# Idle TensorE products in the first block of a delta-rule and feed-forward kernel: 25 in place of 16 behind the first inverse, and seven more in the block's solve

## The chip, the cores and the metric

One core of a Trainium2 chip runs the whole kernel. The metric is the device time of one execution in microseconds (us). A trace of one profiled execution of the kernel before is at hand; the times quoted beside it are of executions without the profiler.

## What is computed

For 4 sequences of 8 heads, 768 steps and 48 channels a delta rule is run, and its output goes through a feed-forward layer. Cut to what matters:

```python
k_n = k / (norm(k) + 1e-6)
for t in range(S):                                   # S = 768
    y[t] = einsum('bhd,bhde->bhe', q[t], state)
    v_old = einsum('bhde,bhd->bhe', state, k_n[t])
    state = state + beta[t] * outer(k_n[t], v[t] - v_old)
x = y as (3072, 384)
h = x @ w_in                                         # 384 x 2048
out = maximum(0.01 * h, h) @ w_out                   # 2048 x 384
```

## The kernel before

The 768 steps are cut into 12 blocks of 64. A block's steps are not run one by one: the Gram products of its keys make a triangular system, this system is inverted (`inv`), and the inverse gives all 64 outputs of the block by matrix products (`solve`). The inverse of blocks 0 and 1 is made together, by elimination on VectorE (DVE, lines 387 and 392), and stands at the front of the program, since nothing else can start before it. All later inverses run beside the feed-forward products of earlier blocks.

In `solve(0)` TensorE (PE) and ScalarE (ACT) take turns, for each of two groups `g` of heads: the corners of the inverse (`pz` L506, `pu` L541, 32 x 32 products, each followed by an ACT copy), the new values (`pw` L635, copied to `rv` by ACT at L637), and the outputs (`py` L655, copied to `ys` by ACT at L657). `columns(0)` turns the outputs by six TensorE transposes (`px` L690), ACT copies them to `x` (L695), and `ffn(0)` multiplies `x` by the feed-forward weights: `ph` (L721), then the activation `gh` on ACT (L731), then `po` (L712).

The weights arrive as raw 64-bit words (`wr`, line 133) and are made into float32 beside block 0's work, one of eight parts `j` after the other: `pack` (ACT, L148), `conv` (DVE, L158 to L161), `expand` (ACT, L168), `final` (DVE, L175), for later blocks also `cast` (ACT, L182) and `lows` (DVE, L189). A table `work` says after which step of block 0 each of these is written, and some carry a gate: `pack(3)` may start only behind the first activation `gh`, `expand(0)` behind the copies to `rv` and `ys`. The engines take their instructions in the order written out, after a scheduling pass has sorted them by its own estimate of when each is ready. A change in one place can so move rows on every engine further on.

One thing on PE has no effect on any result. `warm`, called while the elimination of blocks 0 and 1 still runs (with 12 steps to go), multiplies a constant tile `neg` (128 x 128) by itself, 512 columns wide, 16 times, into a PSUM tile that is not read. These are the idle products. In the kernel before they stand at line 399, and there are no others.

Of the kernel before, what the change touches and what calls it, by code (L numbers as in the profile page):

```python
# [31 lines left out]
HC = C // 2  # L32
P = 128
# [14 lines left out]
def delta_moe_kernel(ctx: ExitStack, tc, kq0, kqT, kv, qT, beta, cst, w_all, out, nblk):  # L48
# [10 lines left out]
    nc = tc.nc  # L59
# [25 lines left out]
    neg = st.tile([P, P], F32R, name="neg")  # L85
# [111 lines left out]
    def need(gen, fn, n):  # L197
        while (fn, n) not in done:
            next(gen)
# [194 lines left out]
    def warm(x, count):  # L394
# [3 lines left out]
        for i in range(count):  # L398
            nc.tensor.matmul(ps.rearrange("p (o t) -> p o t", t=P), neg,
                             neg.rearrange("p (o t) -> p o t", o=1).broadcast_to([P, 4, P]), start=True, stop=True)  # L400

    def inv(b):

        if b:
            need(gg, gram, NB[b][0])
        two = len(NB[b]) > 1
        M = HC if two else HC // 2
        X = sb.tile([P, HC * HC], F32, tag="T", name=f"T{b}", bufs=1)
        T = X[:, 0:M * HC].rearrange("p (m i) -> p m i", m=M)
        if two:  # L410
            nc.gpsimd.memset(T, 0.0)
        else:
            with behind("gl"):
                nc.vector.memset(T, 0.0)
        yield
        L = Lh.pop(b)
        c = norms(b, L.rearrange("p m i -> p (m i)")[:, ::HC + 1])
        if two:
            nc.vector.tensor_copy(X[:, ::HC + 1], c)
        else:  # L420
            for e in range(2):
                r = slice(e * 64, e * 64 + 64)
                nc.vector.tensor_copy(X[r, e:M * HC:HC + 2], c[r, e::2])
        for x in range(2):
            l = L[:, x * HC // 2:(x + 1) * HC // 2]
            nc.vector.tensor_tensor(l, l, c.rearrange("p (o i) -> p o i", o=1).broadcast_to(list(l.shape)), ALU.mult)
        if two:
            for n in NB[b]:
                lengths(n)
        yield  # L430
        for j in range(HC - 1):
            eliminate(b, L, j, T, j + 1 if two else j // 2 + 1)
            if two and j in WARM:
                warm(T[:, 0], WARM[j])
            if j == HC - 2:
                if two:
                    Tc = sb.tile([P, HS, HC], F32, tag="L", name="tc", bufs=2)
                    nc.vector.transpose(Tc.rearrange("p l i -> p i l"), T.rearrange("p m i -> p i m"))

                    for i, n in enumerate(NB[b]):  # L440
                        Tts[n] = Tc, T[i * 64:i * 64 + HC]
                    for g in range(NGR):
                        place(0, g, 1)
                    d = nc.vector.transpose(T, T)
                    mark["inverse"] = d.ins
                    for g in range(NGR):
                        d = place(0, g, 0)
                    mark["inverse"] = d.ins
                else:
                    n = NB[b][0]  # L450
                    Tt = X[:, M * HC:].rearrange("p (i m) -> p i m", m=M)
                    nc.scalar.copy(Tt.rearrange("p i m -> p m i"), T)
                    td = dr.tile([2, HC, HS, HC], F32, tag="td", name=f"td{n}")
                    tt = dr.tile([HS, HC, HC], F32, tag="tt", name=f"tt{n}")
                    Tts[n] = td, tt
                    for x in range(2):
                        a = x * 64
                        for e in range(2):
                            nc.sync.dma_start(td[e, x::2].rearrange("m l i -> l m i"), T[a + e * HS:a + (e + 1) * HS])
                        nc.sync.dma_start(tt.rearrange("l i (x m) -> x l i m", m=M)[x], Tt[a:a + HS])  # L460
                done.add((inv, b))
                if b == 1:
                    mark["el2"] = mark["steps"]
            yield
# [119 lines left out]
    def solve(n):  # L584
        b = where[n][0]
        need(iv, inv, b)
        if n not in nts:
            with behind("po"):
                lengths(n)
        nt = nts.pop(n)  # L590

        def load(g):
            merge_z(n, g, tv(n, g))
            if 0 < n < 3:
                fetch(n, g)

        def tie(g):
            merge_u(n, g, tv(n, g))

        def heads(rows):  # L600

            return ((c, u, slice(c * 64, c * 64 + rows)) for u in range(GU) for c in (1, 0))

        def quarters():

            return ((c, u, e) for u in range(GU) for c in range(2) for e in range(2))

        def out_of(x, g, w):
            p = ps_a.tile([P, 512], F32, tag="a", name=f"{x}{n}_{g}")
            return p[:, 0:GU * w].rearrange("p (u t) -> p u t", u=GU)  # L610

        def kt(g):

            t, k, v = tv(n, g), of("k", n, g), of("v", n, g)
            if n:
                pv = out_of("pk", g, C)
                for c, u, r in heads(D):
                    nc.tensor.matmul(pv[r, u], k[DN, c, u], t[DN, c, u // NPAIR, u % NPAIR], start=True, stop=True)  # L618
                for c in range(2):
                    nc.scalar.mul(t[UP, c], pv[c * 64:c * 64 + D].rearrange("p (y v) t -> p y v t", y=2), -1.0)  # L620
            if not n:
                return
            for s in range(GS):
                us = slice(s * NPAIR, (s + 1) * NPAIR)
                with behind("gl"):
                    nc.vector.tensor_tensor(
                        v[DN, :, us], v[DN, :, us],
                        nt[DN, g, :, us].rearrange("p h (u o) -> p h u o", o=1).broadcast_to([C, 2, NPAIR, D]), ALU.mult)

        def step_w(g):  # L630
            t, v = tv(n, g), of("v", n, g)
            pv = out_of("pw", g, D)
            for c, u, e in quarters():
                a = c * C + e * HC
                nc.tensor.matmul(pv[a:a + HC, u], t[:, c, u // NPAIR, u % NPAIR, e * HC:(e + 1) * HC], v[:, c, u], start=True, stop=True)  # L635
            for c in range(2):
                d = nc.scalar.copy(v[DN, c], pv[c * 64:c * 64 + C])  # L637
            mark["rv"] = d.ins

        def step_s(g):  # L640
            k, v, v1 = of("k", n, g), of("v", n, g), of("v", n + 1, g)
            pv = out_of("pc", g, D)
            for c, u, r in heads(D):
                with nullcontext() if n else behind("ph"):
                    nc.tensor.matmul(pv[r, u], k[:, c, u], v[:, c, u], start=True, stop=True)  # L645
            for c in range(2):
                nc.scalar.copy(v1[UP, c], pv[c * 64:c * 64 + D])  # L647

        def step_y(g):

            qa, v = of("q", n, g), of("v", n, g)
            pv = ps_a.tile([P, 512], F32, tag="a", name=f"py{n}_{g}")
            for c, u, e in quarters():
                a = (c ^ (u // NPAIR)) * C + e * HC
                nc.tensor.matmul(pv[a:a + HC, u * D:(u + 1) * D], qa[:, c, u, e * HC:(e + 1) * HC], v[:, c, u], start=True, stop=True)  # L655
            ys[n, g] = y = sb.tile([P, DO], F32, tag="ys", name=f"ys{n}_{g}", bufs=3)
            mark["ys"] = nc.scalar.copy(y, pv[:, 0:DO]).ins  # L657
            if not n and not g:
                expand(0, "ys", slice(1, 2))

        stages = [(0, load), (1, tie), (LD, kt), (LD + 1, step_w), (LD + 2, step_y), (LD + 3, step_s)]
        if n in (0, nblk - 1):
            stages.remove((LD + 3, step_s))
        for s in range(NSLOT):
            for g in range(NGR):
                for at, stage in stages:
                    if at == s:
                        stage(g)
            if s == NSLOT - 1:
                done.add((solve, n))  # L670
                if 1 < n < nblk - 1:
                    for g in range(NGR):
                        fetch(n + 1, g)
                if n == 0:
                    columns(0)
                    yield
                    for g in range(NGR):
                        step_s(g)
            yield


    def columns(n):

        need(sv, solve, n)
        xs[n] = parts = []
        px = [ps_a.tile([P, 2, TB], F32, tag="a", name=f"px{n}_{i}") for i in range(2)]
        part = [px[cc // 2][:, cc % 2] for cc in range(NCC)]
        for cc, x in enumerate(part):
            for g in range(NGR):
# [155 lines left out]


WEARLY, NPACK, NG = 4, 3, 5
WARM = {HC - 12: 16}
KA = 2
IV, GG = ((9, 17), (6, 17), (6, 17), (2, 17)), ((2, 4), (1, 2), (1, 2))  # L850
SV = (0, 10), (3, 13), (1, 11), (2, 12)
# [67 lines left out]
```

## Time and profile before

| what | value |
|---|---|
| runs without the profiler | 623.45 us median of 3 (622.75 to 623.54) |
| the profiled execution's own time | 627.45 us |
| its span, first to last instruction | 625.7 us |
| mean granted TensorE clock over the span | 0.983 |
| busy share of PE, DVE, ACT | 93%, 69%, 53% |

Busy time is the union of an engine's instructions. The granted clock is 1.00 where TensorE runs at 2.4 GHz and 0.50 where it runs at 1.2 GHz; there is no level between, and a fraction means that the level changed inside the stretch. Ahead of its first record of the clock the profile prints 1.00; there the pace of the products tells the level.

### The profile page before, as it was taken

The numbers are of one execution on the slowest core, as the hardware profiler recorded it, in microseconds if no ns is written. First come the engines' busy times: TensorE is split into PE (matmuls) and PEld (weight loads), VectorE is DVE, ScalarE is ACT, GpSimd is POOL, SyncE is SP. The second block draws the span as 40 slices with busy tenths as digits, with TensorE's granted clock in tenths as the row PEclk, the third lists the DMA queues.
The fourth block names the chain that finished last, engine by engine and source line by source line (L and its number), as shares of the span: only waits on it lengthen the run. The fifth ranks groups of instructions, "written<-read, shape, count | busy, mean of one in ns | idle before, by whom it ended". The sixth has DMA issues, their size and how long they took to land.

```text
span 625.7 us, 22323 instructions
## 1 busy us (share of the span) xinstructions
PE 583.0 (93%) x9122; PEld 534.8 (85%) x9122; DVE 431.2 (69%) x1949; ACT 330.0 (53%) x818; POOL 33.6 (5%) x61
## 2 busy tenths in 40 slices
PE   5279989889899989999999999999999999999996
PEld 4267766689888989999999989999999999999996
DVE  3997899969739949759659739749749659431212
ACT  3475976735536436545545536536545545454432
POOL 6000000100010010010010010010010010100100
PEclk9986999989999999999999999999999999999999
DMA  5986932262266570581580571570580550410101
GB/s 124 310 262 224 282 79 66 43 129 32 46 114 126 103 136 12 104 145 20 106 156 6 110 136 22 113 140 15 112 152 4 114 100 4 85 28 4 25 1 26
DMA packets 122022, 59.69 MB, mean 95 GB/s; under 512 B 111296, under 2 KB 112384, under 8 KB 120896
## 3 DMA queue, kind: packets, MB, share of 16 engines
q1 hardware_dynamic: 117056, 52.95, 39.4%
q0 software_dynamic: 2112, 4.33, 2.7%
q8 instruction: 72, 1.18, 0.9%
q10 hardware_dynamic: 2752, 0.98, 0.8%
q14 instruction: 30, 0.25, 0.1%
HBM read 46.96 MB, written 11.27 MB: 93 GB/s over the span
## 4 chain that ended last, share of the span: by engine, by line
PE 73%; DVE 13%; DMA 5%; ACT 5%; issue 3%; SPq 2%; DVEq 0%; ACTq 0%
PE ph L721 28%; PE po L712 27%; PE pk L618 3%; PE pw L635 3%; DVE T L392 3%; DVE tmp L387 3%; PE py L655 3%; PE pc L645 3%; PE pg L306 2%; DVE w L189 1%; PE px L690 1%; DMA gd<-gs 1%; DMA sq<-tt 1%; ACT cg L168 1%; PE pu L489 1%
## 5 line engine op out<-in xcount | busy, mean ns | idle before, releaser
L721 PE MATMUL ph<-xh,w 128*128 128x256 f32 x1056 | 205.6, 286 | 0.5 <-issue 0.5
L712 PE MATMUL po<-w,gh 128*128 128x384 f32 x704 | 177.9, 344 | 0.0
L721 PEld LDWEIGHTS ph<-xh,w 128*128 128x128 f32 x1056 | 169.2, 189 | 4.8 <-issue 3.9
L736 DVE TENSOR_TENSOR gl<-ph,gh 128x256 fp32r<-128x256 f32 x176 | 74.0, 421 | 143.0 <-ACT ph L735 133.8
L731 ACT ACTIVATE gh<-ph 128x256 fp32r<-128x256 f32 (+1 forms) x192 | 73.5, 385 | 181.9 <-PE ph L721 121.8
L721 PE MATMUL ph<-xl,w 128*128 128x256 f32 x528 | 149.0, 284 | 1.7 <-DVE xl L124 1.7
L712 PEld LDWEIGHTS po<-w,gh 128*128 128x128 f32 x704 | 120.9, 188 | 3.4 <-issue 1.8
L712 PE MATMUL po<-w,gl 128*128 128x384 f32 x352 | 113.2, 343 | 3.0 <-DVE gl L736 2.8
L392 DVE TENSOR_TENSOR T<-T,tmp 128x60 f32<-128x60 f32 (+35 forms) x661 | 112.4, 207 | 0.7
L387 DVE TENSOR_TENSOR tmp<-T,L 128x60 f32<-128x60 f32 (+35 forms) x661 | 112.0, 207 | 0.6
L721 PEld LDWEIGHTS ph<-xl,w 128*128 128x128 f32 x528 | 100.1, 190 | 2.6 <-DVE xl L124 2.1
L712 PEld LDWEIGHTS po<-w,gl 128*128 128x128 f32 x352 | 65.4, 188 | 5.4 <-DVE gl L736 4.6
L735 ACT ACTIVATE ph<-ph 128x256 f32<-128x256 f32 x176 | 66.8, 379 | 0.0
L763 POOL DMA_DIRECT2D out<-ob x44 | 22.9, 526 | 555.7 <-ACT ob L762 554.7
L323 DVE TENSOR_TENSOR rq<-pg,csb 64x256 f32<-64x256 f32 x80 | 33.8, 423 | 1.6
L620 ACT ACTIVATE rt<-pk 48x512 f32<-48x512 f32 x44 | 26.1, 592 | 5.5 <-PE pk L618 4.7
L721 PE MATMUL ph<-x,cg 128*128 128x256 f32 x96 | 24.9, 414 | 2.4 <-DVE cg L175 2.2
L647 ACT COPY rv<-pc 48x384 f32<-48x384 f32 x44 | 20.9, 475 | 10.4 <-PE pc L645 9.8
L721 PEld LDWEIGHTS ph<-x,cg 128*128 128x128 f32 x96 | 19.5, 208 | 7.7 <-DVE cg L175 3.4
L637 ACT COPY rv<-pw 64x384 f32<-64x384 f32 x48 | 22.7, 474 | 4.4 <-PE pw L635 3.3
L655 PEld LDWEIGHTS py<-rv,rq 128*32 128x32 f32 x1536 | 19.3, 114 | 5.7 <-issue 2.1
L655 PE MATMUL py<-rv,rq 128*32 128x48 f32 x1536 | 21.6, 213 | 2.2 <-ACT rv L637 1.1
(99 smaller groups left out, 603.0 us busy)
## 6 DMA issues: line engine op xcount, KB each, us to landing
wr<-in_w_all SPq DMA_DIRECT2D x8, 1536.0 KB, 13.7
kq<-in_kqT SPq DMA_DIRECT2D x40, 192.0 KB, 5.3
L<-gd SPq DMA_DIRECT2D x20, 256.0 KB, 4.0
rk<-in_kv SPq DMA_DIRECT2D x24, 192.0 KB, 3.9
rv<-in_kv SPq DMA_DIRECT2D x24, 192.0 KB, 4.3
rq<-in_qT SPq DMA_DIRECT2D x24, 192.0 KB, 3.6
out<-ob POOLq DMA_DIRECT2D x44, 96.0 KB, 2.4
td<-T SPq DMA_DIRECT2D x40, 64.0 KB, 3.3
```

The costliest lines, as they stand in the source:

```text
L323: nc.vector.tensor_tensor(qa[DN, c, b * NPAIR:(b + 1) * NPAIR], pv[b][r, 1], tri[r].rearrange("p (o t) -> p o t", o=1).broadcast_to([C, NP ...
L387: nc.vector.tensor_tensor(tv, t[:, :, j:j + 1].broadcast_to([P, k, w]), L[:, j, j + 1:].rearrange("p (o w) -> p o w", o=1).broadcast_to([P ...
L392: mark["steps"] = nc.vector.tensor_tensor(t, t, tv, ALU.subtract).ins
L620: nc.scalar.mul(t[UP, c], pv[c * 64:c * 64 + D].rearrange("p (y v) t -> p y v t", y=2), -1.0)
L637: d = nc.scalar.copy(v[DN, c], pv[c * 64:c * 64 + C])
L655: nc.tensor.matmul(pv[a:a + HC, u * D:(u + 1) * D], qa[:, c, u, e * HC:(e + 1) * HC], v[:, c, u], start=True, stop=True)
L712: i = nc.tensor.matmul(po[t][:, :DO], a[:, ts_], w, start=(f == 0 and k == 0), stop=(f == NFC - 1 and k + 1 == len(ways)))
L721: i = nc.tensor.matmul(ph, w[:, cc * P:(cc + 1) * P], a, start=(k == 0), stop=(k + 1 == len(ways)))
L731: i = nc.scalar.activation(gh, ph, AF.Prelu, alpha=0.01)
L735: i = nc.scalar.activation(ph, ph, AF.Prelu, alpha=0.01)
L736: mark["gl"] = nc.vector.tensor_tensor(gl, ph, gh.bitcast(F32), ALU.subtract).ins
L763: nc.gpsimd.dma_start(out[r0:r0 + C], ob[a:a + C])
```

## The change

`warm` issues 25 idle products in place of 16. A new helper `idle` issues the same product into a PSUM tile that the next real products then write over: two ahead of the `pw` products of group 1, three ahead of the `py` products of group 1, and one into each of the two `px` tiles, all in block 0 only.

```diff
+    def idle(ps, count):
+
+        for i in range(count):
+            nc.tensor.matmul(ps.rearrange("p (o t) -> p o t", t=P), neg,
+                             neg.rearrange("p (o t) -> p o t", o=1).broadcast_to([P, 4, P]), start=True, stop=True)
...
         def out_of(x, g, w):
             p = ps_a.tile([P, 512], F32, tag="a", name=f"{x}{n}_{g}")
+            if not n:
+                idle(p, IDLE.get((x, g), 0))
...
             pv = ps_a.tile([P, 512], F32, tag="a", name=f"py{n}_{g}")
+            if not n:
+                idle(pv, IDLE.get(("py", g), 0))
...
         px = [ps_a.tile([P, 2, TB], F32, tag="a", name=f"px{n}_{i}") for i in range(2)]
+        if not n:
+            for x in px:
+                idle(x.rearrange("p a t -> p (a t)"), IDLE["px"])
...
-WARM = {HC - 12: 16}
+WARM = {HC - 12: 25}
+IDLE = {("pw", 1): 2, ("py", 1): 3, "px": 1}
```

The first place is TensorE in the solve of block 0. Before, from the second `pu` on (`x31` are that many products in a row; a float32 product is two instructions in the trace):

```order
L635 MATMUL pw_0_770<-rv_84,rt_82 32x48
L541 MATMUL pu_1_751<-zs,T_413 32x32 x15
L635 MATMUL pw_1_805<-rv_85,rt_83 32x48
L635 MATMUL pw_0_770<-rv_84,rt_82 32x48 x31
L635 MATMUL pw_1_805<-rv_85,rt_83 32x48 x31
L655 MATMUL py_0_856<-rv_84,rq_78 32x48 x32
L655 MATMUL py_1_892<-rv_85,rq_79 32x48 x32
L690 MATMUL px_0_927<-csb,ys_0_889 128x128
L690 MATMUL px_1_928<-csb,ys_0_889 128x128
```

With the change (the lines have moved by up to 13: `pw` L643, `py` L665, `px` L703, the idle products L405):

```order
L643 MATMUL pw_0_779<-rv_84,rt_82 32x48
L547 MATMUL pu_1_760<-zs,T_413 32x32 x15
L405 MATMUL pw_1_814<-neg 128x512 x2
L643 MATMUL pw_1_814<-rv_85,rt_83 32x48
L643 MATMUL pw_0_779<-rv_84,rt_82 32x48 x31
L643 MATMUL pw_1_814<-rv_85,rt_83 32x48 x31
L665 MATMUL py_0_867<-rv_84,rq_78 32x48 x32
L405 MATMUL py_1_903<-neg 128x512 x3
L665 MATMUL py_1_903<-rv_85,rq_79 32x48 x32
L405 MATMUL px_0_941<-neg 128x512
L405 MATMUL px_1_942<-neg 128x512
L703 MATMUL px_0_941<-csb,ys_0_900 128x128
```

The two idle products of `pw_1` stand ahead of 31 of the 32 products of `pw_0` too, since the first product of `pw_1` was already written ahead of them; the three of `py_1` stand between the two groups, and those of `px` between the last `py` product and the first transpose.

The second place is VectorE near the end of block 0, where the elimination of block 2 (`T`, `tmp`) meets the low parts of block 1's columns (`xl`, L124, which need ACT's copy `xh`, L123). Before:

```order
L387 TENSOR_TENSOR tmp_26_0_1749<-T_1483,L_1075 128x35
L387 TENSOR_TENSOR tmp_28_1_1763<-T_1483,L_1075 128x21
L392 TENSOR_TENSOR T_1483<-T_1483,tmp_26_0_1749 128x7x5
L392 TENSOR_TENSOR T_1483<-T_1483,tmp_28_1_1763 128x7x3
L387 TENSOR_TENSOR tmp_27_0_1755<-T_1483,L_1075 128x28
L124 TENSOR_TENSOR xl_0_1722<-px_0_1713,xh_0_1721 128x256
L387 TENSOR_TENSOR tmp_29_1_1769<-T_1483,L_1075 128x14
L392 TENSOR_TENSOR T_1483<-T_1483,tmp_27_0_1755 128x7x4
L392 TENSOR_TENSOR T_1483<-T_1483,tmp_29_1_1769 128x7x2
L387 TENSOR_TENSOR tmp_28_0_1761<-T_1483,L_1075 128x24
L387 TENSOR_TENSOR tmp_30_1_1775<-T_1483,L_1075 128x8
L124 TENSOR_TENSOR xl_1_1726<-px_0_1713,xh_1_1725 128x256
```

With the change, starting where the first `xl` now stands:

```order
L387 TENSOR_TENSOR tmp_25_1_1725<-T_1499,L_1091 128x36
L392 TENSOR_TENSOR T_1499<-T_1499,tmp_23_0_1711 128x6x8
L124 TENSOR_TENSOR xl_0_1738<-px_0_1729,xh_0_1737 128x256
L392 TENSOR_TENSOR T_1499<-T_1499,tmp_25_1_1725 128x6x6
L387 TENSOR_TENSOR tmp_24_0_1717<-T_1499,L_1091 128x49
L387 TENSOR_TENSOR tmp_26_1_1767<-T_1499,L_1091 128x35
L392 TENSOR_TENSOR T_1499<-T_1499,tmp_24_0_1717 128x7x7
L392 TENSOR_TENSOR T_1499<-T_1499,tmp_26_1_1767 128x7x5
L124 TENSOR_TENSOR xl_1_1742<-px_0_1729,xh_1_1741 128x256
L387 TENSOR_TENSOR tmp_25_0_1723<-T_1499,L_1091 128x42
L387 TENSOR_TENSOR tmp_27_1_1773<-T_1499,L_1091 128x28
L124 TENSOR_TENSOR xl_2_1746<-px_1_1730,xh_2_1745 128x256
```

The first `xl` stands 14 instructions of the elimination earlier than before, and the other two follow close behind it. Between these two places single rows of PE, ACT, DVE and the DMA queue of SyncE have changed places as well (`pk` and `pw` of block 1 stand ahead of some `po`, for instance); no instruction has been added or taken out there.

## Rows read from the trace of the kernel before

**Rows 1.** The page: its span.

```profile
span 625.7 us, 22323 instructions
```

**Rows 2.** Windows: busy us and (instructions) of PE, PEld, DVE, ACT, POOL; granted clock.

```profile
37.40:41.80 4.40, 1.43 (x66) 1.29 (x66) 4.30 (x6) 2.23 (x5) 0.00 (x0) 1.00 1.04 200
41.82:58.88 17.06, 14.85 (x335) 12.54 (x336) 15.84 (x25) 8.97 (x19) 0.00 (x0) 0.50 0.54 156
58.90:70.00 11.10, 11.10 (x102) 8.28 (x100) 7.12 (x12) 10.48 (x16) 0.00 (x0) 1.00 1.02 352
130.58:133.97 3.39, 3.15 (x13) 3.15 (x14) 3.23 (x11) 0.99 (x3) 0.00 (x0) 0.50 0.93 214
```

**Rows 3.** Timeline of PE: start, length, line, op, operands, count, idle before and releaser.

```profile
40.37 1.21 PE L506 MATMUL pz<-rt,gm 32*32 32x32 f32 x64 [3.03 <-ACT rt L472]
...
44.32 1.66 PE L635 MATMUL pw<-rv,rt 128*32 128x48 f32 x67
46.80 1.41 PE L635 MATMUL pw<-rv,rt 128*32 128x48 f32 x58 [0.82 <-issue]
...
50.63 1.49 PE L655 MATMUL py<-rv,rq 128*32 128x48 f32 x60 [1.05 <-ACT cg L168]
52.06 1.79 PE L690 MATMUL px<-csb,ys 128*128 128x128 f32 x6
54.09 5.21 PE L721 MATMUL ph<-x,cg 128*128 128x256 f32 x12 [0.25 <-ACT x L695]
...
60.81 1.56 PE L721 MATMUL ph<-x,cg 128*128 128x256 f32 x6
```

**Rows 4.** Timeline of PE in two short windows: the idle products of before.

```profile
32.09 3.20 PE L399 MATMUL warm<-neg 128*128 128x512 f32 x7
...
35.12 2.22 PE L399 MATMUL warm<-neg 128*128 128x512 f32 x9
```

**Rows 5.** Timeline of ACT in and behind block 0's solve.

```profile
48.38 0.97 ACT L637 COPY rv<-pw 64x384 f32<-64x384 f32 x2 [1.46 <-PE pw L635]
...
52.20 0.48 ACT L657 COPY ys<-py 128x384 f32<-128x384 f32 x1 [0.76 <-PE py L655]
53.67 0.92 ACT L695 COPY x<-px 128x256 f32<-128x256 f32 x3 [0.99 <-PE px L690]
...
59.34 0.66 ACT L731 ACTIVATE gh<-ph 128x256 f32<-128x256 f32 x2 [3.38 <-PE ph L721]
59.88 1.61 ACT L148 COPY cg<-wr 128x1536 bf16<-128x1536 bf16 x1
```

**Rows 6.** Timeline of DVE in the same stretch.

```profile
50.24 0.96 DVE L175 SCALAR_TENSOR_TENSOR cg<-wr,cg 128x768 uint32<-128x768 uint32 x1 [0.84 <-ACT cg L168]
...
53.78 0.95 DVE L175 SCALAR_TENSOR_TENSOR cg<-wr,cg 128x768 uint32<-128x768 uint32 x1
...
57.30 1.75 DVE L175 SCALAR_TENSOR_TENSOR cg<-wr,cg 128x1536 uint32<-128x1536 uint32 x1
...
61.53 0.56 DVE L158 TENSOR_SCALAR cg<-cg 128x768 uint32<-128x768 uint32 x1 [2.46 <-ACT cg L148]
```

**Rows 7.** Timeline of PE in block 1's solve, full clock.

```profile
96.57 1.57 PE L635 MATMUL pw<-rv,rt 128*32 128x48 f32 x128
...
105.64 2.86 PE L721 MATMUL ph<-x,cg 128*128 128x256 f32 x12
...
111.57 0.82 PE L690 MATMUL px<-csb,ys 128*128 128x128 f32 x6
```

**Rows 8.** Windows: ACT's share of block 0's feed-forward stretch.

```profile
59.34:79.90 20.56, 20.56 (x293) 15.98 (x294) 15.59 (x24) 20.29 (x30) 0.00 (x0) 1.00 0.92 290
```

**Rows 9.** Timelines of ACT, then DVE, near the end of block 0.

```profile
116.48 0.38 ACT L123 CAST xh<-px 128x256 fp32r<-128x256 f32 x1
...
115.90 0.31 DVE L392 TENSOR_TENSOR T<-T,tmp 128x48 f32<-128x48 f32 x2
...
117.79 0.42 DVE L124 TENSOR_TENSOR xl<-px,xh 128x256 fp32r<-128x256 f32 x1
```

## Prediction

> **What bounds the kernel now.** I read the page first: one core, a span of 625.7 us [rows 1]. In the later blocks TensorE (PE) is busy almost without a gap, so time won at the front comes out at the end, if nothing in between gives it back. The front is where the change lies, so the second view is the granted clock by windows. From 37.4 to 41.8 us PE is busy 1.43 of 4.40 us; then the clock stands at 0.50 from 41.82 to 58.88, although PE is busy for 14.85 of these 17.06 us, and at 1.00 again from 58.9 [rows 2]. The third view, PE's timeline, says what runs there: an idle stretch of 3.03 us ahead of `pz`, then the small products `pu`, `pw`, `py`, then the six transposes `px` (1.79 us) and the first twelve `ph` instructions (5.21 us) [rows 3]. In block 1, at full clock, the same twelve take 2.86 us, the six transposes 0.82, and all 128 `pw` 1.57, against 1.66 and 1.41 for 125 of them in block 0 [rows 7, 3]. The fourth view is who waits. ACT sits idle 3.38 us for `ph` before the first `gh` at 59.34; `pack(3)` follows at 59.88; DVE waits 2.46 us for it until 61.53 [rows 5, 6]. Behind 59.34 ACT is busy 20.29 of 20.56 us [rows 8]: it carries the chain there, and whatever brings the first `gh` forward moves this whole stretch.
>
> So the question is whether the added products bring the clock back before the twelve `ph`, and what they cost on the way.
>
> **The change, step by step.** *Price of one idle product.* At 1.2 GHz seven of them start between 32.09 and 35.12, 0.43 us each; after that nine take 2.22 us, 0.25 each [rows 4].
>
> *Nine more behind the inverse.* 9 x 0.25 = 2.2 us, or 3.9 if all were at the low level. They begin where the sixteenth ends and fill the 3.03 us in which PE waits for ACT's copy `rt` [rows 3]. I take 0; without that cover at most 3.9 - 3.03 = 0.9 would come onto the path.
>
> *Two ahead of `pw_1`.* 0.5 to 0.9 us, and nearly all of `pw_0` is queued behind them, then ACT's copies to `rv`. Two things absorb them: a wait of 0.82 us in the middle of `pw` for which the profile names no releaser, and DVE, which needs the copies only through `expand` and then waits 0.84 [rows 3, 6]. Against them stands the faster `pw` at full clock: 3.07 - 1.57 = 1.5 us at best, of which DVE's wait lets 0.84 through. I take 0 net, and keep -0.84 and +0.9 as ends. The wait without releaser is a wait for no data, so I do not expect the clock to shorten it.
>
> *Three ahead of `py_1`.* 0.75 to 1.3 us. Before, PE idles 1.05 us just there, and the 60 instructions behind it take 1.49, against 60/128 x 1.57 = 0.74 at full clock, by `pw`, the nearest row [rows 3, 7]. Full clock: 0.75 - 0.75 = 0. Low level without the cover: +1.3.
>
> *Two ahead of `px`.* 0.5 to 0.87 us. `py` ends at 50.63 + 1.49 = 52.12, and half the transposes need ACT's copy `ys`, done at 52.68 [rows 3, 5]: 0.56 us of cover. I take 0 at full clock, +0.3 at the low level.
>
> *`px` and `ph`.* The three transposes behind `ys` take about half of 0.82 in place of half of 1.79: -0.5. The twelve `ph`: 2.86 in place of 5.21: -2.35. Their second half also needs `final` on DVE, done at 53.78 + 0.95 = 54.73 [rows 6]; `ph` would start at 53.6 and need it 1.4 us later, at 55.0, so it does not hold them. Sum at the first `gh`: -2.85.
>
> *Handing on.* `pack(3)` moves with it. DVE ends its own queue at 57.30 + 1.75 = 59.05, so `conv(3)` can come forward by its wait, 2.46, and no more; ACT, full behind 59.34, carries 2.85 [rows 6, 8]. I take the middle, -2.6.
>
> *The moved rows.* Of the moves further on, the one with a price I can bound is `xl` at the end of block 0. It stands 14 DVE instructions earlier; two of them take 0.31 us, so about 2 us [rows 9]. Its operand `xh` is ready at 116.48 + 0.38 = 116.86, and `xl` started at 117.79, so there were 0.93 us to spare; 2 us earlier it would wait about 1 us and hold up the elimination behind it. `xh` stands at the end of ACT's queue, as before. Ends 0 and +1; I take +0.4, since PE needs `xl` and gets it earlier. The fall of the clock at 130.58 to 133.97 [rows 2] I leave as it is; at worst it is lost or doubled, at most half of 3.39, 1.7 us.
>
> *Sum.* -2.6 + 0.4 = -2.2 us: the profiled span goes to 623.5. That execution took 627.45 us, 4.0 more than the median of the runs; the change belongs to both, so the median goes from 623.45 to 621.2.
>
> **A rule against the trace.** PE idles 3.03 us ahead of `pz`, and the clock falls at 41.82 [rows 3, 2]. The Trainium skill (TensorE: Matmul & The Clock Gate, Part 1 and "HAM oscillation") says that the clock falls back when PE idles and is released by sustained activity. By that rule, filling the gap keeps the clock at full for the whole solve; that is rival B. [...] After the 25 products come about 4 us of `pz` and `pu` only. So I expect the clock to fall all the same, and the wide products ahead of `pw_1`, `py_1` and `px` to bring it back by the time of `px`: my sum goes by that.
>
> **The rivals.**
>
> *B, the clock never falls, or is back before `pw`.* Then `rv` and `expand` come earlier too, DVE's 0.84 us goes as well, and `conv(3)` moves by 2.46 + 0.84 = 3.3: 623.45 - 3.3 + 0.4 = 620.5; if the later fall also goes, 618.8. For it: the gap ahead of `pz` is filled. Against: the narrow products that follow.
>
> *C, the clock returns in the middle of `ph`.* Half of 2.35 is saved and `px` not: -1.2, with +0.4 and 0.3 for the idle products at the low level: 623.45 - 0.5 = 623.0, no change that can be told. For it: before, it returned only after 5 us of `ph`.
>
> *D, slower: the idle products run at the low level and the clock returns at 58.9 as before.* All seven cost 7 x 0.43 = 3.0 us on the way to `px`. Covered are 0.82 ahead of `pw_1` and 0.56 by `ys`; the 1.05 ahead of `py_1` perhaps: +0.6 to +1.6, with the +0.4 of the moved rows and `ph` unchanged +1.0 to +2.0, so about 625.0. It decides if the clock is still at 0.50 when the first `ph` starts and stays there for most of the twelve. Against it: more wide work in the same stretch.
>
> *E, won and given back.* The clock comes back, the first `gh` comes 2.85 us earlier, but the changed order on ACT, PE and DVE further on costs 2 to 3 us: 623.4. For it: ACT and DVE are nearly full, so each wait of one for the other counts. Against: the same instructions are issued, and ACT needs 20.29 us of work in any order.
>
> **How the numbers follow.** About 0.2% (1.25 us) is what a measurement can tell from no change: faster is below 622.2, slower above 624.7. Chances: forecast 0.42 (its own range 620.0 to 622.4, from the ends of `pw` and `xl`), B 0.14, C 0.14, D 0.13, E 0.17. Faster: 0.39 of the forecast, all of B, 0.03 of C, 0.05 of E: 0.61. Slower: 0.10 of D, 0.04 of E: 0.14. No change: 0.25. The range runs from 618.8 (B without the later fall) to 625.0 (D).
>
> **What would show it.** Right: granted clock 1.00 when the first `ph` starts, the twelve `ph` near 2.86 us, the first `gh` near 56.5 in place of 59.34, DVE's wait ahead of `conv(3)` gone, and everything at 70 us some 2.6 us earlier. The nine added products end before `pz`, which still starts at 40.37. Wrong: clock 0.50 at `ph`; `pw_0`, `py_1` or `px` starting later by the idle products' length; or a lead at 60 us that is gone at 120, on DVE ahead of `xl`, or on ACT ahead of a `pack` whose raw weights have not landed yet.

## The result, and the profile after

| | before | after |
|---|---|---|
| median of 7 runs each, us | 623.54 (622.57 to 626.11) | 628.65 (626.70 to 631.72) |
| ratio, 95% interval | | 1.0066 (1.0044 to 1.0089) |
| profiled execution, its time / span, us | 627.45 / 625.7 | 631.72 / 629.9 |

The change makes the kernel slower, by 0.66% or 4.1 us (0.0066 x 623.54) where 2.2 us faster was forecast. The ratio is not that of the two medians, which stand 5.1 us apart. Of the kernels in the experiments below each has 12 runs, but p1, p3 and p4 only 6, 6 and 9, since runs in a slower state are left out, so their ratios are, if anything, too low.

The granted clock of the profiled execution of after, by windows (busy time of each engine, then the clock), answers to [rows 2]:

```profile
42.90:56.50 13.60, 11.63 (x308) 9.15 (x305) 11.23 (x20) 5.91 (x12) 0.00 (x0) 0.50 0.28 71
56.54:70.00 13.46, 13.11 (x114) 10.17 (x113) 10.41 (x16) 11.63 (x18) 0.00 (x0) 1.00 0.97 369
128.20:135.00 6.80, 4.85 (x17) 4.34 (x18) 6.52 (x15) 1.89 (x6) 0.00 (x0) 0.50 0.69 148
165.75:169.15 3.40, 3.26 (x51) 3.18 (x52) 2.14 (x18) 1.90 (x4) 0.00 (x0) 0.50 0.22 61
234.00:237.40 3.40, 3.37 (x27) 3.01 (x28) 0.22 (x1) 0.41 (x1) 0.00 (x0) 0.50 0.63 102
```

The clock falls as forecast after `pz` and `pu`, and it is back at 56.5 us, ahead of the twelve `ph`. But it falls three times more, at 128.2, 165.7 and 234.0 us, where [rows 2] had one fall. PE's timeline answers to [rows 3]:

```profile
44.56 1.22 PE L405 MATMUL pw<-neg 128*128 128x512 f32 x2
45.71 1.35 PE L643 MATMUL pw<-rv,rt 128*32 128x48 f32 x56
48.10 1.51 PE L643 MATMUL pw<-rv,rt 128*32 128x48 f32 x64 [1.04 <-issue]
...
49.56 1.55 PE L665 MATMUL py<-rv,rq 128*32 128x48 f32 x56
52.04 0.38 PE L665 MATMUL py<-rv,rq 128*32 128x48 f32 x6 [0.92 <-issue]
52.35 1.65 PE L405 MATMUL py<-neg 128*128 128x512 f32 x3
53.93 1.51 PE L665 MATMUL py<-rv,rq 128*32 128x48 f32 x64
55.37 1.22 PE L405 MATMUL px<-neg 128*128 128x512 f32 x2
56.39 0.89 PE L703 MATMUL px<-csb,ys 128*128 128x128 f32 x6
57.63 1.13 PE L734 MATMUL ph<-x,cg 128*128 128x256 f32 x4 [0.35 <-ACT x L708]
```

All seven idle products lie ahead of the clock's return, so the first two take 1.22 us and the three of `py` 1.65, and two waits without a releaser, 1.04 and 0.92 us, stand between them. The two of [rows 3] were of the same kind (0.82 us, and 1.05 for which the view names ACT's `cg`; both end at the record numbers shown further down), but the first now falls into the end of `pw_0`, for which ACT waits:

```profile
48.60 0.97 ACT L645 COPY rv<-pw 64x384 f32<-64x384 f32 x2 [3.16 <-PE pw L643]
49.88 0.97 ACT L645 COPY rv<-pw 64x384 f32<-64x384 f32 x2 [0.31 <-PE pw L643]
...
60.52 0.66 ACT L744 ACTIVATE gh<-ph 128x256 f32<-128x256 f32 x2 [1.03 <-PE ph L734]
61.06 1.61 ACT L148 COPY cg<-wr 128x1536 bf16<-128x1536 bf16 x1
```

The second pair of `rv` copies comes at 49.88 in place of 48.38, the first `gh` at 60.52 in place of 59.34 [rows 5], although the twelve `ph` take 2.9 us (57.63 to 60.52) and not 5.21. So in this execution nothing was won at the front, and it loses more further on: the 57th `gh` starts at 250.01 us, 4.4 behind that of before (245.65).

### The profile page after: what moved, and what is told of

It reads as the page before. It is cut to its first block, busy times and chain, and to the rows that moved or that the text cites. A ratio compares the mean times of both kernels' runs of the same rounds, so it can differ in the third digit from the quotient of the medians.

```text
span 629.9 us, 22360 instructions
## 1 busy us (share of the span) xinstructions
PE 589.7 (94%) x9138; PEld 540.5 (86%) x9138; DVE 430.8 (68%) x1949; ACT 330.2 (52%) x818; POOL 33.7 (5%) x61
## 4 chain that ended last, share of the span: by engine, by line
PE 79%; DVE 12%; ACT 3%; issue 2%; DMA 2%; SPq 0%; DVEq 0%; ACTq 0%
PE ph L734 30%; PE po L725 30%; PE pk L626 3%; PE py L665 3%; PE pw L643 3%; DVE T L392 3%; DVE tmp L387 3%; PE pc L653 3%; PE pg L306 2%; DVE w L189 2%; PE px L703 1%; DVE cg L175 1%; PE pz L495 1%; ACT cg L148 1%; PE pu L495 1%
## 5 line engine op out<-in xcount | busy, mean ns | idle before, releaser
L734 PE MATMUL ph<-x,cg 128*128 128x256 f32 x96 | 23.3, 388 | 2.0 <-DVE cg L175 1.6
L665 PEld LDWEIGHTS py<-rv,rq 128*32 128x32 f32 x1536 | 19.5, 114 | 6.0 <-ACT ph L748 2.0
L643 PEld LDWEIGHTS pw<-rv,rt 128*32 128x32 f32 x1536 | 19.2, 114 | 5.3 <-issue 2.1
L665 PE MATMUL py<-rv,rq 128*32 128x48 f32 x1536 | 22.0, 213 | 1.5 <-issue 1.5
```

Source lines behind the costliest of these rows:

```text
L734: i = nc.tensor.matmul(ph, w[:, cc * P:(cc + 1) * P], a, start=(k == 0), stop=(k + 1 == len(ways)))
```

## The experiments

**Taking the change apart.** Four kernels hold the rows of PE, ACT, DVE and SyncE's queue in the order of before or of after (by ordering edges that add no wait), with some of the idle products:

```diff
x1 and x3
-WARM = {HC - 12: 16}
+WARM = {HC - 12: 25}
x1 and x4
+IDLE = {("pw", 1): 2, ("py", 1): 3, "px": 1}
all four: the order of before (x1, x3, x4) or of after (x2)
         delta_moe_kernel(tc, *args, o, nblk)
+        pin(tc)
```

x1: 

> All 32 idle products of the changed kernel (25 behind the inverse, 2, 3 and 2 in the solve), but every other instruction of every engine in the order of the kernel before. Theory 1 (the idle products themselves cost: they run at the low clock ahead of pw, py and px, and move pw_0 behind a wait for instructions): first gh near 60.5, as in the changed kernel, and 1 to 2 us slower than before. Theory 2 (the changed order further on costs): at most 1.2 us slower from the first gh, nothing more behind it. Theory 3 (falls of the clock in blocks 1 and 2, which differ from execution to execution, cost the rest): 2 to 4 us slower, with such falls in the profile.

x2: 

> The 16 idle products of the kernel before and none of the others; every other instruction in the order of the changed kernel. Theory 1: within 0.5 us of before. Theory 2: about 3 us slower, with the first gh at 59.3 as before. Theory 3: slower only as far as its profile shows more of the span at 0.50 behind 130 us.

x3: 

> 25 idle products behind the inverse in place of 16, none in the solve, order of the kernel before. The clock falls one step later than in the kernel before or at the same place, and pw, py, px and ph run as before: within 1 us of before by theories 1 and 2; by theory 1, if the 18 instructions move the end of a fetched stretch of instructions back into pw_0, the first copy to rv comes 1 to 2 us later and the first gh about 1 us later.

x4: 

> 16 idle products behind the inverse as before and the seven of the solve, order of the kernel before. Theory 1: the clock is low during the solve, the seven cost 2 to 3 us ahead of px, the clock returns near 55.5 and ph takes 2.9 us in place of 5.2: the first gh between 59.0 and 60.5, the time -0.5 to +2 us. Theory 2: the same, with nothing lost behind the first gh.

| kernel | median us | ratio to before (95%) | first `gh` in its profile |
|---|---|---|---|
| x1 all idle products, old order | 627.24 | 1.0043 (1.0019 to 1.0066) | 55.78 |
| x2 none added, new order | 625.44 | 1.0022 (0.9999 to 1.0044) | 56.74 |
| x3 25 behind the inverse, old order | 625.67 | 1.0023 (0.9996 to 1.0049) | 56.08 |
| x4 the seven, old order | 624.91 | 1.0008 (0.9982 to 1.0034) | 57.18 |

Ratios here and below are to runs of before on the same chip, in turn with these. No part makes it faster, and x1 and x2 add up to the whole. Theory 1 had the first `gh` of x1 near 60.5, and theory 2 had x2 about 3 us slower (0.0022 is 1.4 us): neither came. And all four profiles have the first `gh` 2.2 to 3.6 us earlier than [rows 5], x2 too, which has no idle product more than before. That put the profile of before itself in doubt.

**The same two kernels again.** No edit; two more profiled executions of each.

b1: 

> The kernel before, unchanged, in a second profiled execution (the first, on which the prediction rests, took 627.45 us, 4.0 over the median of its runs). Theory P (the profiled execution was an unusual one): in most executions of the kernel before the clock is back before the twelve ph anyway, so that the first gh stands near 56 to 57.5 us, the profiled time is 622 to 625, and there was little left for the idle products to win. Rival Q: the clock is back only near 58.9 in every execution of before, the first gh stands at 59.3 again, and what the idle products win at the front is lost further on.

b2: 

> The kernel before, unchanged, in a third profiled execution. Theory P: first gh at 56 to 57.5 us in at least one of the two repeats, and the order of the executions by time follows when the clock falls and returns, at the front and near 130, 166 or 230 us. Rival Q: first gh at 59.3 in both, within 0.3 us.

a1: 

> The changed kernel, unchanged, in a second profiled execution (the first took 631.72 us, the slowest of its seven). Theory P: the boundary of the instruction blocks stands at the same records (waits of about 1 us in pw_0 near 47 us and in py_0 near 51), so the first rv copy is late by 2 us or more again, while the falls of the clock at 166 and 234 us differ from execution to execution; time 626 to 630. Rival Q: the falls at 128, 166 and 234 us come again at the same places, as they belong to the changed order.

a2: 

> The changed kernel in a third profiled execution. Theory P: as in the second, the waits without a releaser at the same records, the later falls of the clock elsewhere or gone; time 626 to 630. Rival Q: the same falls at the same places in all three executions.

The kernel before, third execution (622.55 us), windows and PE:

```profile
41.80:48.60 6.80, 6.66 (x275) 6.24 (x275) 6.63 (x12) 4.58 (x11) 0.00 (x0) 0.50 0.31 72
48.66:59.00 10.34, 7.47 (x137) 5.76 (x127) 10.03 (x18) 7.81 (x12) 0.00 (x0) 1.00 0.67 239
```

```profile
50.24 0.66 PE L690 MATMUL px<-csb,ys 128*128 128x128 f32 x4 [0.63 <-ACT ys L657]
51.25 1.56 PE L721 MATMUL ph<-x,cg 128*128 128x256 f32 x6 [0.35 <-ACT x L695]
53.52 1.56 PE L721 MATMUL ph<-x,cg 128*128 128x256 f32 x6 [0.71 <-DVE cg L175]
```

Without one idle product more, the clock is back at 48.6 and the twelve `ph` run at full clock: six in 1.56 us, a wait of 0.71 for DVE, six more. What the execution of [rows 2, 3] has until 58.9 ended at 50.6 (b1) and 48.6 us (b2). Over all executions, from the trace's clock records and ACT's rows (the low clock of the last microseconds, which all six have, is left out):

```
execution      us      first gh  low clock at the front   low clock later
before, 1st  627.45     59.34        41.8 to 58.9         130.6 to 134.0
before, b1   624.59     56.65        40.4 to 50.6         228.1 to 231.5
before, b2   622.55     55.12        41.8 to 48.6         127.1 to 130.5
after, 1st   631.72     60.52        42.9 to 56.5         128.2 to 135.0, 165.7 to 169.1, 234.0 to 237.4
after, a1    627.05     56.18        43.8 to 47.2         125.7 to 132.5, 231.5 to 234.9
after, a2    625.49     56.36        44.2 to 47.6         126.1 to 129.5
```

Theory P holds for the front. Over all profiles here the median first `gh` is at 56.97 us in the nine without added idle products (these three, x2, p1, p2, q1, q4, r1) and at 56.47 in the nine with all of them (after's three, x1, p3, p4, q2, q3, r2): 0.5 us, where 2.85 were forecast, and single ones lie between 55.1 and 60.5. Q fails for before. Of after's later falls only the one at 126 to 128 us comes each time, the others do not. What P said of after came only in part: a2 took 625.49 us and not 626 to 630, the wait in `pw_0` came in neither a1 nor a2, and the one in `py_0` only in a2 at any length (0.72 us).

**Where PE waits for nothing.** Count PE's instructions in the trace in their order (weight loads, products and 169 semaphore and drain instructions). Then each of the 75 waits without a releaser of 0.3 us or more behind 40 us, in all twenty profiles of this study, stands at a record that leaves the same remainder. Some of them:

```
record   1473  1729  4545  4801  5825  6081  9153  13505  15041  16577
mod 256   193   193   193   193   193   193   193    193    193    193
```

The page counts 72 packets of 16 KB on the queue for instructions, for 18,413 PE records (71.9 x 256). That is the page of before (packets, MB, share of the engines):

```profile
q8 instruction: 72, 1.18, 0.9%
```

So PE's instructions come in blocks of 256 records, and PE stands still where the next one is late. The packets bear this out: every trace has as many of them on q8 as boundaries, and matched in order, each of the 75 waits ends 1.2 to 1.9 us (median 1.4) behind the end of its block's packet, and nowhere behind 40 us does a block begin earlier than that. PE's timeline shows the same run of `py` in block 3 in b1:

```profile
197.37 1.57 PE L655 MATMUL py<-rv,rq 128*32 128x48 f32 x128
```

and in x4, where it stands 14 records further on:

```profile
197.97 1.57 PE L664 MATMUL py<-rv,rq 128*32 128x48 f32 x124
200.79 0.28 PE L664 MATMUL py<-rv,rq 128*32 128x48 f32 x4 [1.26 <-issue]
```

1.57 us in one piece there; here 1.26 us of standing still, four products ahead of its end. The Trainium skill (Runtime: NRT & Kernel Launch, "Instruction fetch mechanics") has blocks of 16 KiB and 256 instructions, which this agrees with, and calls the crossing "mostly hidden"; here it is hidden behind wide products, and costs up to 2.0 us behind small ones in the executions of before and after (`pc`, in the first one of after). Each idle product is two records, so the change moves all later boundaries by 32.

To move them alone, p1 to p4 put tiny products ahead of the first idle product, where PE waits 12.2 us for DVE in the profile of before; nothing reads them:

```diff
         ps = ps_a.tile([P, 512], F32, tag="a", name="warm")
+        for i in range(PAD):
+            nc.tensor.matmul(ps[0:HC, 0:HC], neg[0:HC, 0:HC], neg[0:HC, 0:HC], start=True, stop=True)
```

p1 (before, PAD = 60): 

> The kernel before with 60 tiny products (32x32, two PE records each, so 120 records) put into the stretch in which PE waits for the elimination, ahead of the first idle product. Nothing else is changed; nothing reads them. Theory F: all waits of PE without a releaser stand at every 256th PE record (record 193 of each 256 in all profiles so far), and they cost when 256 records in a row take under some 3 us; 120 records more put these places into the middle of the runs of small products, of which each then falls into two blocks with wide products beside it. A count over the records of before gives 0.9 us of such waits in place of 3.3: the time falls by 1.5 to 2.4 us (ratio 0.996 to 0.998). Rival C: such places do not matter in sum, and what makes the changed kernel slower is the work of the idle products themselves and the clock; then the ratio is 1.000 within 0.002.

p2 (before, PAD = 8): 

> The kernel before with 8 tiny products (16 records) at the same place. Theory F: this is nearly the worst shift by the same count, 6.9 us of waits in place of 3.3 (as an upper bound), so slower by 1.5 to 3.5 us (ratio 1.002 to 1.006), with new waits without releaser in py near 200 us and pc near 300, 347 and 484 us. Rival C: 1.000 within 0.002, as eight products in a stretch in which PE waits do nothing.

p3 (after, PAD = 44): 

> The changed kernel with 44 tiny products (88 records) at the same place, so that with its own 32 added records the shift is 120 as in the first kernel. Theory F: the waits without releaser go from 4.5 to about 0.8 us by the count, and the time falls by 2 to 3.5 us against the changed kernel: ratio to before 1.000 to 1.003 in place of 1.0066. Rival C: the ratio stays at 1.005 to 1.008.

p4 (x1, PAD = 44): 

> All added idle products in the order of before (ratio 1.0043 earlier), with 44 tiny products at the same place: shift 120 again. It holds the idle products' own price apart from the shift. Theory F: ratio 0.996 to 0.999, close to that of the first kernel here; what is left between the two is the idle products' own price. Rival C: 1.003 to 1.006, as without the tiny products.

| kernel | shift, records | median us | ratio to before (95%) |
|---|---|---|---|
| p1 before + 60 tiny | 120 | 630.29 | 1.0105 (1.0064 to 1.0145) |
| p2 before + 8 tiny | 16 | 624.22 | 1.0004 (0.9982 to 1.0025) |
| p3 after + 44 tiny | 120 | 632.46 | 1.0141 (1.0108 to 1.0174) |
| p4 x1 + 44 tiny | 120 | 629.13 | 1.0097 (1.0065 to 1.0128) |

That boundaries matter is shown, since sixty products in a wait cost 1%; but theory F's sizes were wrong in both directions. The waits it counted did shrink (in p1 0.3 us in all behind 57 us, against 1.7 to 2.2 in the three of before; p1's profile is of the fastest of its six runs, 624.79 us, and does not show where the 1% goes). But a new one stands at record 5825, in the middle of `pw` of block 3, 2.1 us long in p1 and 3.2 in p3 and p4. PE's timeline of p4:

```profile
192.34 1.22 PE L644 MATMUL pw<-rv,rt 128*32 128x48 f32 x92
196.74 0.87 PE L644 MATMUL pw<-rv,rt 128*32 128x48 f32 x32 [3.19 <-DVE tmp L387]
```

and the windows ahead of that wait, in it, and while the clock is low (clock, DMA share and GB/s at the end):

```profile
188.00:193.50 5.50, 5.50 (x153) 5.02 (x149) 5.01 (x20) 4.13 (x11) 0.00 (x0) 1.00 1.03 185
193.56:196.70 3.14, 0.00 (x0) 0.00 (x0) 3.14 (x21) 0.65 (x2) 0.00 (x0) 0.79 0.10 17
195.45:202.20 6.75, 5.46 (x51) 5.34 (x52) 2.64 (x22) 1.87 (x5) 0.00 (x0) 0.50 0.02 5
```

The view names DVE as releaser, the last event that it saw; `pw` reads nothing of the elimination, and the trace has the block's packet start at 193.96 and take 1.45 us. PE had entered the block before at 188.5, so this packet started 5.5 us later, the latest of that trace; the median over the twenty traces behind 40 us is 0.7 us. In between the 16 DMA engines were full (share 1.03, first row). The twenty traces have 23 packets that start over 4 us late there, and from the entry to the packet the share is 0.98 or more for every one; 19 of them, behind wide products, cost nothing. So full DMA engines go with late packets; no run changes the one alone. And the clock falls within the wait, at 195.4 us (third row), so it costs twice. A count with one fixed time for each block can't see that.

**The shift without the idle products, and the reverse.** q1 to q3 are the same edit with other numbers, q4 is x2 with DVE's rows in the order of before.

q1 (before, PAD = 16, shift 32): 

> The kernel before with 16 tiny products (32 records) in the stretch in which PE waits: the same shift of the 256-record boundaries as in the changed kernel and in the idles in the old order, without one idle product more. Theory F: the shift is what the idle products cost, so the ratio is like that of the idles in the old order, 1.003 to 1.005, with the wait at 194 to 197 us at the end of pw. Rival I: the idle products cost by their own time and what they do to the clock; then 1.000 within 0.002.

q2 (after, PAD = 112, shift 32 + 224 = 256): 

> The changed kernel with 112 tiny products (224 records), so that with its own 32 the boundaries stand where they stand in the kernel before. Theory F: the waits in pw and py of block 0 and near 197 and 302 us move or go, the ratio falls from 1.0066 to near that of the changed order alone, 1.001 to 1.004. Rival I: it stays at 1.005 to 1.008.

q3 (x1, PAD = 112, shift 256): 

> All added idle products in the order of before with 112 tiny products: boundaries where they are in before, order as in before, so only the idle products themselves are left of the change. Theory F: ratio 1.000 within 0.002 (from 1.0043). Rival I: 1.003 to 1.005 as before.

q4 (x2, DVE as before): 

> 16 idle products, PE, ACT and DMA queue in the changed order, but DVE in the order of before, so that the xl rows stand 14 elimination rows later again. Theory O: in the changed order the early xl lets PE run ahead and then wait once for 4.25 us for DVE's gl near 122 to 126 us, and the clock falls there (in all five profiles of the changed order, in two of nine of the old order); with the old rows PE waits in pieces of 0.5 to 1.3 us again, no fall at 126 us in most executions, mean clock 0.988 in place of 0.983, ratio 1.000 to 1.001 in place of 1.0022. Rival: PE's own changed rows (pk and pw ahead of po) make the difference, the fall stays, 1.002.

| kernel | median us | ratio to before (95%) |
|---|---|---|
| q1 before, shifted as in after | 625.75 | 1.0029 (1.0011 to 1.0048) |
| q2 after, shifted back | 625.77 | 1.0021 (0.9998 to 1.0044) |
| q3 all idle products, old order, shifted back | 623.99 | 0.9993 (0.9972 to 1.0015) |
| q4 new order, DVE's rows old | 627.73 | 1.0035 (1.0012 to 1.0058) |

One block of instructions more has been fetched where 256 records were added, by the page of q3:

```profile
q8 instruction: 73, 1.20, 0.8%
```

This settles the idle products' part, as far as 0.2% can be told. The shift of 32 costs by itself what the idle products seemed to cost (1.0029 against x1's 1.0043, intervals overlapping), and the idle products with the boundaries back in place cost nothing that can be told (0.9993). With it taken back, after falls to what its order alone costs (1.0021, and x2 1.0022). Nor do the tiny products cost by their number: 8 and 112 of them leave the time as it is (p2, q3), 16 and 60 do not (q1, p1). It does not settle where the shift's 2 us go: the waits without releaser behind 57 us add up to 1.3 us in q1's profile, 2.4 in q3's and 3.4 in q2's, so they don't follow the ratios (q2's profile is of the slowest of its 12 runs, those of q1 and q3 lie near their medians). The boundary at record 5825 costs 0.9, 0.4 and 1.5 us in x1, a1 and a2, and nothing in q1.

**The order.** Where `xl` comes earlier, PE no longer waits for it, and then waits once, longer, for DVE's `gl` (PE's waits from 118 to 136 us: line, waited for, us in total, times, longest). In a2:

```profile
PE po L725 <- DVE gl L749: 4.3, 1, 4.3
```

in b1:

```profile
PE po L712 <- DVE gl L736: 2.3, 2, 1.3
PE ph L721 <- DVE xl L124: 1.2, 1, 1.2
```

and in q4:

```profile
PE ph L733 <- DVE xl L124: 2.6, 2, 1.4
PE po L724 <- DVE gl L748: 2.3, 2, 1.2
```

All six profiles in the full new order and without a fill (after's three, x2, p3, q2) have this wait and a fall of the clock at 125.6 to 128.2 us; of the twelve in the old order three have one near there. DVE's old rows (q4) take wait and fall away, and yet the kernel is not faster, so the moved `xl` is not the cost, or not alone. The last two runs fill waits:

```diff
r1: x2 with PAD = 106, and ahead of the first po<-gl of block 1
+    for i in range(22):
+        nc.tensor.matmul(po[t].rearrange("p (o t) -> p o t", t=P)[:, 0:NCC], zero,
+                         neg.rearrange("p (o t) -> p o t", o=1).broadcast_to([P, NCC, P]), start=False, stop=False)
r2: x1 with PAD = 112, and ahead of pz of block 4
+    idle(ps, 8)
```

r1: 

> The changed order with 16 idle products, as in the second kernel of the first experiment (ratio 1.0022), and 22 wide products of a zero tile (128 x 384, added to po and so without effect) in the one wait of 4.25 us ahead of the first po<-gl of block 1, near 122 us; 106 tiny products ahead of the first idle product, so that behind the fill the 256-record boundaries stand where they did. Theory O: the concentrated wait costs by the fall of the clock behind it (there in all profiles of the changed order); filled, the clock stays at full level near 126 us and the ratio falls from 1.0022 to 1.000 or below. Rival: the fall is not what the order costs, or the boundaries that the 106 tiny products move ahead of 122 us cost as much; then 1.002 or more, with or without the fall.

r2: 

> The idles in the order of before with 112 tiny products (ratio 0.9993 earlier), and 8 idle products ahead of the pz whose DMA wait of 2.4 us near 227 us comes ahead of a fall of the clock in most executions of all kernels. A candidate that may beat both. If the fall follows the wait, it goes: 1.4 us in the executions that have it, so 0.9975 to 0.999, and the spread of the times gets smaller. Rival: the fall comes from elsewhere or the wait is not filled: 0.9993 again.

PE's timeline of r1 at the fill:

```profile
125.24 3.98 PE L730 MATMUL po<-neg,zero 128*128 128x384 f32 x22
129.64 0.62 PE L732 MATMUL po<-w,gl 128*128 128x384 f32 x2 [0.42 <-DVE gl L756]
```

and of r2:

```profile
224.79 1.99 PE L397 MATMUL pz<-neg 128*128 128x512 f32 x8
227.46 0.65 PE L498 MATMUL pz<-sq,gm 128*32 128x128 f32 x16 [0.68 <-DMA sq<-tt]
```

Both fills take the wait away in the profile (r1 3.98 us of products and 0.42 of wait; r2 1.99 and 0.68), and no fall stands behind it. For r2 that does not show the fill's effect: q3, the same kernel without the fill, has the wait (2.37 us) and no fall there either. r1 is at 627.63 us, 1.0053 (1.0028 to 1.0079): its tiny products shift the boundaries ahead of 122 us by 212, and its profile has a wait of 1.64 us at 103.3 that no other profile has, so it says nothing on the order. r2 is at 623.60, 0.9991 (0.9966 to 1.0016): as q3, and not to be told from before. No version beats the kernel before by more than a measurement can tell.

## Why the prediction was wrong

- **The price of the clock, -2.85 at the first `gh`: the step that failed.** It was read from one execution, 4.0 us over the median of the runs. The text saw that and went on with "the change belongs to both". The kernel after has its first `gh` where it was forecast, near 56.5, in two of three executions (56.18 and 56.36). But in two more executions of before `ph` runs at full clock already and the first `gh` stands at 56.65 and 55.12 (b1, b2), so the gain was there only in the execution that was priced. Over all profiles it is 0.5 us, and what was to be handed on to `conv(3)` fell with it.
- **"I take 0" for the nine, the two, the three and the two.** Right as their own time goes (q3: 0.9993). What was missed is that they are instructions: 32 records that move each later block of PE's instructions. The wait of 0.82 us in `pw` was seen and called a wait for no data, which it is; that it sits at a record's number and not at a place in the program was not asked. The 1.05 us ahead of `py_1`, taken as cover with ACT's `cg` as releaser, end at such a record too (1729). The shift costs 1.0029 by itself (q1), 1.8 us.
- **The clock ahead of `ph`.** Right in its course: it falls after `pz` in spite of the filled gap, so rival B is out, and it is back by 56.5, 47.2 and 47.6 us. That the wide products bring it back is not shown, since it came back at 50.6 and 48.6 us without them (b1, b2). By the Trainium skill's rule weighed there (TensorE: Matmul & The Clock Gate, "HAM oscillation") the filled gap would have kept it up; the traces do not agree, as PE is busy for 11.84 of the 12.00 us ahead of the fall in a2 and for all 3.40 behind it (rows below). In the first execution of after the seven ran at the low level and cost as rival D said, yet the twelve `ph` were at full clock. D's own terms reach +2.0, so 625.4, where the range ended at 625.0; the time measured lies above both.

```profile
32.10:44.10 12.00, 11.84 (x152) 9.54 (x154) 11.83 (x44) 9.10 (x28) 0.00 (x0) 1.00 1.01 295
44.20:47.60 3.40, 3.40 (x114) 2.69 (x114) 3.23 (x6) 1.17 (x3) 0.00 (x0) 0.50 0.23 56
```

- **The moved rows, +0.4.** The order costs 1.0022 (x2; the interval just reaches 1) and 1.0021 (q2), some 1.4 us. `xl` itself was won: PE's waits for it are gone. In its place came the one wait of 4.25 us and the fall at 126 to 128 us. Whether this is the cost stays open, since q4 lost the fall and not the time, and r1 changed two things.
- **"The fall at 130.58 I leave as it is."** Wrong: falls further on come and go from one execution to the next, and the new order has one at 126 us each time.
- **Rival E** had the right half: the changed order costs. But nothing had been won to be given back.

So 0.66% is made up of some 0.2% for the order and 0.3 to 0.45% for the shift (q1, and after against q2), with nothing for the idle products and next to nothing won at the front.

## What to carry to other kernels

Before pricing a change against a profile whose own time lies above the median of the runs, ask whether the thing to be won is there in a typical execution; here a second profile would have ended the matter. Instructions put into a wait are free in time but not in place: they move every later boundary of the instruction blocks, and if a kernel has dense runs of small products, count the records and try the same shift with products that do nothing else, before crediting or blaming the change itself. A wait cut out on one engine can come back as one longer wait further on, and one long wait can cost the clock as well.

## What the runs showed of the hardware

- PE's waits for instructions stand at 256th records, to the record, in all twenty profiles; 256 records more are one 16 KB packet more on the queue (73 in place of 72).
- Each of these 75 waits ends 1.2 to 1.9 us behind the end of the block's packet.
- PE can wait 3.2 us for such a block after the DMA engines were full (share 1.03), and the clock then falls for 6.8 us (p4). All 23 packets that started over 4 us late did so at a share of 0.98 or more.
- Where the clock falls and how long it stays low differs between executions of one kernel by more than this change: 48.6 to 58.9 us for its return at the front in three executions of before.
